# Moving the score, value and x-transpose steps of three attention blocks to other slots of the feed-forward loop

## The chip, the cores and the metric

The kernel runs on one core of a Trainium2 chip. The metric is the time of one execution in microseconds (us) on the device. The kernel before takes 279.12 us as the median of 3 runs (278.87 to 279.75). One further execution was taken with the hardware profiler; all rows quoted here come from it.

## The reference

Two stages are computed one after the other. The inputs q, k and v have 8 batches, 8 heads, 576 positions and 64 channels.

```python
q_c = q.reshape(B, H, nc, chunk, D)          # chunk = 64, so nc = 9
scores = scale * np.matmul(q_c, k_c.transpose(0, 1, 2, 4, 3))
scores = scores - np.max(scores, axis=-1, keepdims=True)
attn = np.exp(scores)
attn = attn / (np.sum(attn, axis=-1, keepdims=True) + 1e-09)
out = np.matmul(attn, v_c)
...
x = np.ascontiguousarray(attn_out.transpose(0, 2, 1, 3)).reshape(B * S, H * D)
h = np.maximum(x @ w_in, 0.0)
return (h * h @ w_out).astype(np.float32)
```

Attention is local to chunks of 64 positions. Its result x has 4608 rows of 512 numbers and goes through a feed-forward network of 2048 hidden units with the square of a relu.

## The kernel before, in words

The 4608 rows are cut into 18 groups of 256 rows, each of four chunks. Two groups make a block, so block n holds groups 2n and 2n+1; there are 9 blocks, 0 to 8. Every step is written in Python, so the program that the engines get is one long list for each of them, and each engine works through its own list from front to back.

For a group the attention consists of three steps on TensorE, which the plan in the code names SC, AV and XT:

- **SC** (`scores`, line 464): 32 matmuls of 64x64 write the scores of the group into a PSUM tile of two banks (line 483). One ScalarE instruction of 128x1024 takes the exponential into an SBUF tile `e` (line 494).
- **AV** (`values`, line 496): two halves, t = 0 and t = 1. In each, 16 matmuls of 64x65 multiply `e` with v (line 510) into a PSUM tile. The 65th column is the sum of the exponentials. VectorE takes its reciprocal (line 442) and multiplies (line 443) into the SBUF tile `x`.
- **XT** (`transpose_x`, line 530): 8 TensorE transposes of 128x128 (line 540) write x transposed into a PSUM tile, and ScalarE copies it into `xT` (line 545), which the feed-forward network reads.

All these PSUM tiles come from `att_bank` (line 358), which in this part of the kernel hands out two tiles in turn, `ps_att` and `ps_att2`. A step that gets a tile has to wait until the last reader of that tile is done: the exponential for scores, the product on line 443 for values, the copy on line 545 for transposes. For the two groups of block 2 and of block 4 the order is SC, SC, AV, AV, XT, XT; in block 3 the first group has its XT before the second has its AV.

Ahead of SC stand the casts of q and k to bf16 (`C`, lines 449 and 454, on GpSimd, for block 4 on ScalarE) and a DMA transpose (`TD`, line 460, issued by SyncE).

The feed-forward network of a block j is `ffn_in(j)` (line 573) and `ffn_out(j)` (line 728). `ffn_in` gives one step for each 128 hidden units: four matmuls into a PSUM tile (line 579), a relu on ScalarE (line 590), and a square, for most steps on VectorE (line 598) and for a few on ScalarE (line 596). Its PSUM tiles come from a pool of four, so a step waits for the relu of the step four before it. In block 1 the two groups go through `ffn_in` apart, 16 steps each of 256 columns; in blocks 2 and 3 together, 16 steps of 512 columns. `ffn_out` multiplies sums and differences of the squares with sums of `w_out`, in 14 steps of 8 matmuls of 128x256 (line 780). VectorE makes the sums (line 614), ScalarE copies intermediate products away (`keep`, line 840), and VectorE adds a kept one to a finished one and stores the sum (`summed_out`, line 820, whose add is again line 614).

The loop `for j in range(QUADS)` (line 1004) weaves both together: after each step of the network, called a slot, it issues what a dictionary `plan` holds for that slot. So with j = 1 the network of block 1 runs while the attention of block 2 is done, with j = 2 the attention of block 3, with j = 3 that of block 4. For j = 1 slots 0 to 31 are `ffn_in` and 32 to 45 `ffn_out`. For j = 2 slots 0 to 15 are `ffn_in`, slots 16 to 18 hold no work of TensorE, and 19 to 32 are `ffn_out`. For j = 3 the loop has the 16 slots of `ffn_in` alone. From block 4 on a different scheme follows (`run`, line 1160), which is not changed.

Of the kernel before, what the change touches and what calls it, by code (L numbers as in the profile page):

```python
# [144 lines left out]
def kernel(  # L145
# [174 lines left out]
    def go(pieces):  # L320
        for f in pieces:
            f()
# [250 lines left out]
    def ffn_in(j, parts):  # L573
        gT = gT_main.rearrange("p (u h) (f t) -> p u h f t", u=2, f=4)
        xT = xTs[j]
        for u, (c, n, ft) in enumerate((c, n, ft) for c, n, fts in parts for ft in fts):
            h = ps_ffn.tile([128, 512], FP32, name="ps_ffn")
            for dt in range(n_dt):
                nc.tensor.matmul(  # L579
                    out=h[:, 0:n],  # L580
                    lhsT=w_in_bf[:, dt, ft * 128:(ft + 1) * 128],
                    rhs=xT[:, c // 128:(c + n) // 128, dt, :],
                    start=(dt == 0), stop=(dt == n_dt - 1))
            if n == 512 or u % 2 == 0:
                state["rl"] = state.get("rl", -1) + 1
                rl_tile = relu_sb[state["rl"] % 4]
                if j < 3:
                    rl_tile = rl_tile.bitcast(BF16)
            rl = rl_tile[:, u % 2 * 512:] if n < 512 else rl_tile
            nc.scalar.activation(out=rl[:, 0:n], in_=h[:, 0:n], func=AF.Relu)  # L590
            u0, u1 = c // GT, (c + n) // GT
            dst = gT[:, u0:u1, ft // 4, ft % 4, :]
            src = rl[:, 0:n].rearrange("p (u t) -> p u t", t=GT)
            if (n == 512 and ft in SQUARES_ON_ACT) or (
                    n < 512 and ft in (12, 3)) or (j == 0 and u == 0):
                nc.scalar.activation(out=dst, in_=src, func=AF.Square)
            else:
                nc.vector.tensor_tensor(out=dst, in0=src, in1=src, op=ALU.mult)  # L598
            yield
# [16 lines left out]
    def summed(out, in0, in1, op=ALU.add):  # L616
        return lambda *_: add(out, in0, in1, op)
# [277 lines left out]
    def ffn_out_by_ft(j):  # L895

        n_tt = BT // 128
        o_ps = [ps_ffn.tile([128, d_model], FP32, name="ps_ffn") for _ in range(n_tt)]

        def mm(tt, ft):  # L900
            nc.tensor.matmul(  # L901
                out=o_ps[tt],
                lhsT=g_piece(j, tt // 2, ft // HF, ft % HF // 4)[
                    :, ft % 4, tt % 2 * 128:tt % 2 * 128 + 128],
                rhs=w_out_bf[:, ft, :],
                start=(ft == 0), stop=(ft == n_ft - 1))


        for ft in range(n_ft - 4):
            for tt in range(n_tt - 1 if ft == 0 else n_tt):  # L910
                mm(tt, ft)
                if ft == 1 and tt == n_tt - 2:
                    mm(n_tt - 1, 0)
            yield
        for tt in range(n_tt):
            for ft in range(n_ft - 4, n_ft):
                mm(tt, ft)
            o_sb = ffn_pool.tile([128, d_model], FP32, name="o_sb", bufs=4)
            nc.scalar.copy(out=o_sb, in_=o_ps[tt])
            b, s0 = chunks[blocks[j][tt // 2]][0]  # L920
            t0 = b * S + s0 + tt % 2 * 128
            nc.gpsimd.dma_start(out=out[t0:t0 + 128, :], in_=o_sb)
            yield
# [3 lines left out]
    def pieces(grps):  # L927
        for g in grps:
            yield from qk_pieces(g)
        for g in grps:  # L930
            yield from v_pieces(g)

    SC, AV, XT = scores, values, transpose_x
    TD = transpose_qk_dma
# [69 lines left out]
    for j in range(QUADS):  # L1004
        grps, nxt, far = blocks[j], blocks[j + 1], blocks[j + 2]
        plan = {}

        def at(slot, f, *x):
            plan.setdefault(slot, []).append((f, x))

        if j == 0:
            loads, go_slots = pieces(far), range(17)
            at(28, summed(b11_p_b21, b11, b21))
            for slot, f in ((24, TA), (27, SC), (29, AV), (31, XT)):
                at(slot, f, nxt[0])
            at(31, TQ, nxt[1])
            at(31, TK, nxt[1])
            at(31, summed(b22_m_b21, b22, b21, ALU.subtract))
            phases = [first_ffn_in, ffn_out_by_ft(0)]
        elif j == 1:  # L1020
            loads, go_slots = itertools.chain(*map(qk_pieces, far)), range(26, 48)
            for slot, f in ((3, SC), (6, AV), (12, XT)):
                at(slot, f, grps[1])
            for i, g in enumerate(nxt):
                for slot, f in ((16 + 4 * i, C), (21 + 4 * i, TD), (36 + i, SC), (38 + 2 * i, AV),
                                (41 + 2 * i, XT)):
                    at(slot, f, g)
            for i, g in enumerate(far):
                at(36 + 4 * i, C, g)
                at(42 + 3 * i, TD, g)  # L1030
            at(2, summed(b12_p_b21, b12, b21))
            at(12, summed(b11_m_b12, b11, b12, ALU.subtract))
            at(20, summed(b12_p_b22, b12, b22))
            out_j = ffn_out(1)
            for i in (20, 27, 29, 31):
                at(i, lambda: next(out_j)())
            phases = [ffn_in(1, [(0, 256, FT_ORDER), (256, 256, FT_ORDER)]), out_j]
        else:
            out_j = ffn_out(j)
            for i in (14, 15):  # L1040
                at(i, lambda: next(out_j)())
            phases = [ffn_in(j, [(0, BT, range(n_ft))])]
            if j == 2:
                loads, go_slots = itertools.chain(*map(v_pieces, nxt), pieces(far)), [
                    *range(16), *range(27, 36)]
                slots = {SC: (6, 10), AV: (12, 22), XT: (15, 28), CQ: (20, 22), CK: (21, 24), TD: (24, 26)}
                for f in (CQ, CK, TD):
                    for i, g in enumerate(far):
                        at(slots[f][i], f, g)
                phases.append(out_j)  # L1050
            else:
                loads, go_slots = pieces(far), range(11)
                at(11, C, far[0])
                at(13, CQ, far[1])
                at(13, TD, far[0])
                slots = {SC: (2, 4), AV: (7, 10), XT: (13, 15)}
            for f in (SC, AV, XT):
                for i, g in enumerate(nxt):
                    at(slots[f][i], f, g)
            if j == 2:  # L1060
                for i, f in enumerate((summed(a21_p_a22, a21, a22),
                                       summed(a12_m_a21, a12, a21, ALU.subtract),
                                       summed(a11_p_a21, a11, a21))):
                    at(1 + 2 * i, f)
        slot = 0
        for phase in phases:
            for _ in phase:
                if slot in go_slots:
                    for f in loads:
                        f()  # L1070
                        break
                for f, x in plan.get(slot, []):
                    f(*x)
                slot += 1
        assert all(x < slot for x in plan), (j, slot, sorted(plan))
        if j < QUADS - 1:
            go(loads)
# [19 lines left out]
    for j in range(QUADS, n_blk):  # L1097
        if j == QUADS:
            n = 14 - LEAD
            slots = [1 + 19 * i // n for i in range(n)]  # L1100
            assert len(slots) == n
        else:
            slots = [s for s in range(4, 20) if s % 16 not in NO_OUT]
# [119 lines left out]
```

## Time and profile before

| | us |
|---|---|
| median of 3 runs | 279.12 |
| profiled execution, its own time | 278.37 |
| its span, first to last instruction | 276.6 |
| TensorE busy | 265.3 (96%) |
| VectorE busy | 199.3 (72%) |
| ScalarE busy | 170.1 (61%) |
| GpSimd busy | 90.7 (33%) |

A row of the timeline reads: start in us from the span's start, duration in us, engine, line of the kernel, operation, output and input, how many instructions are merged in the row, and in brackets how long the engine was idle before it and what ended that. PE is TensorE, PEld its weight loads, DVE is VectorE, ACT is ScalarE, POOL is GpSimd, SP is SyncE. The ends of matmuls are modelled, so the start of the next row tells more than the duration. The 1.8 us between the profiled execution's time and its span lie before the first and behind the last instruction.

### The profile page before, as it was taken

How to read it: one execution, taken by the hardware profiler on the slowest of the kernel's cores; microseconds unless marked ns; L12 is line 12 of the kernel's file. 1: busy time of each engine (PE TensorE's matmuls, PEld its weight loads, DVE VectorE, ACT ScalarE, POOL GpSimd, SP SyncE). 2: the span in 40 equal slices, each digit the busy share in tenths (PEclk: the TensorE clock that was granted, in tenths of full speed). 3: DMA queues.
4: the chain of work that ended last, by engine and by line, in shares of the span. 5: the costliest groups of instructions: out<-in, count | busy, mean ns of one | idle time of the engine just before them, and what ended most of it. 6: DMA issues, size and time to landing. Idle time of an engine off the chain costs nothing.

```text
span 276.6 us, 7949 instructions
## 1 busy us (share of the span) xinstructions
PE 265.3 (96%) x3274; PEld 203.9 (74%) x3277; DVE 199.3 (72%) x365; ACT 170.1 (61%) x302; POOL 90.7 (33%) x122
## 2 busy tenths in 40 slices
PE   2889999999999999999999999999999999999994
PEld 2764445888774588447888888888898888888884
DVE  1457415999538692599989998799679877994852
ACT  1657514894458883867678765566856664756430
POOL 2048734350270012140245224551434312431600
PEclk9999999999999999999999999999999999999999
DMA  7999999999999999998999999697995330220223
GB/s 216 260 373 383 366 318 262 325 209 162 278 209 206 245 246 231 285 240 121 229 228 199 217 236 198 116 214 198 254 195 162 78 76 2 89 62 9 71 83 114
DMA packets 133943, 55.07 MB, mean 199 GB/s; under 512 B 102160, under 2 KB 129808, under 8 KB 133904
## 3 DMA queue, kind: packets, MB, share of 16 engines
q1 hardware_dynamic: 131136, 46.02, 70.9%
q0 software_dynamic: 2624, 8.39, 9.7%
q8 instruction: 26, 0.43, 0.6%
q10 hardware_dynamic: 144, 0.13, 0.1%
q14 instruction: 13, 0.11, 0.1%
HBM read 36.70 MB, written 9.44 MB: 167 GB/s over the span
## 4 chain that ended last, share of the span: by engine, by line
PE 82%; DVE 8%; DMA 4%; SPq 4%; issue 1%; ACT 0%; POOL 0%
PE ps_ffn L657 23%; PE ps_out L780 22%; PE ps_ffn L579 13%; PE ps_ffn L780 12%; PE ps_ffn L901 5%; DVE gT L598 4%; PE ps_att L510 2%; DMA w_st<-in_moe_w_in_dram 2%; PE ps_att L483 2%; PE ps_att L540 2%; DMA qkT<-qkb 2%; SPq L266 1%; SPq L308 1%; SPq L312 1%; DVE x L443 1%
## 5 line engine op out<-in xcount | busy, mean ns | idle before, releaser
L579 PE MATMUL ps_ffn<-xT,w_in_bf 128*128 128x512 bf16 (+1 forms) x328 | 58.0, 333 | 0.1
L780 PEld LDWEIGHTS <-w_st 128*128 128x128 bf16 x512 | 48.8, 98 | 6.6 <-DVE w_st L614 0.5
L665 DVE CUSTOM_DVE_ANT_0 relu<-ps_ffn,w_st 128x512 f32<-128x512 f32 x60 | 39.3, 685 | 12.8 <-PE ps_ffn L657 11.4
L598 DVE TENSOR_TENSOR gT<-relu 128x256 bf16<-128x256 bf16 (+2 forms) x68 | 34.6, 543 | 18.0 <-ACT relu L590 17.5
L579 PEld LDWEIGHTS <-w_in_bf 128*128 128x128 bf16 x328 | 31.1, 98 | 21.4 <-POOL w_in_bf L334 0.2
L590 ACT ACTIVATE relu<-ps_ffn 128x256 bf16<-128x256 f32 (+2 forms) x82 | 39.5, 502 | 10.3 <-PE ps_ffn L579 9.6
L657 PE MATMUL ps_ffn<-qk_st,w_in_bf 128*128 128x256 bf16 x240 | 35.3, 273 | 0.0
L657 PEld LDWEIGHTS <-w_in_bf 128*128 128x128 bf16 x320 | 30.6, 98 | 4.0 <-issue 0.3
L809 POOL DMA_DIRECT2D out_dram<-o_sb x24 | 17.6, 733 | 44.7 <-DVE o_sb L614 24.6
L780 PEld LDWEIGHTS <-gT 128*128 128x128 bf16 x296 | 28.6, 98 | 3.3
L780 PE MATMUL ps_out<-w_out_bf,w_st 128*128 128x256 bf16 x240 | 30.8, 273 | 0.0
L699 ACT ACTIVATE w_st<-ps_ffn 128x512 f32<-128x512 f32 x20 | 11.9, 598 | 27.5 <-PE ps_ffn L657 27.5
L443 DVE TENSOR_TENSOR x<-ps_att,recs 128x512 bf16<-128x512 f32 x36 | 24.9, 692 | 1.2
L657 PEld LDWEIGHTS <-qk_st 128*128 128x128 bf16 x240 | 22.6, 98 | 2.9
L676 POOL TENSOR_TENSOR qk_st<-relu 128x512 bf16<-128x512 f32 x10 | 10.3, 1034 | 41.6 <-DVE relu L665 38.1
L657 PE MATMUL ps_ffn<-xT,qk_st 128*128 128x256 bf16 x160 | 23.9, 273 | 0.0
L494 ACT ACTIVATE e<-ps_att 128x1024 bf16<-128x1024 f32 x18 | 18.4, 1023 | 8.6 <-PE ps_att L483 8.6
L676 POOL TENSOR_TENSOR gT<-relu 128x512 bf16<-128x512 f32 x10 | 10.3, 1033 | 36.9 <-DVE relu L665 36.9
L449 POOL CAST qkb<-qk_st 128x1024 bf16<-128x1024 f32 x12 | 14.8, 1236 | 13.3 <-DMA qk_st<-in_q_dram 13.3
L674 ACT ACTIVATE gT<-relu 128x512 bf16<-128x512 f32 x28 | 17.7, 631 | 0.0
L780 PE MATMUL ps_ffn<-w_out_bf,w_st 128*128 128x256 bf16 x144 | 17.7, 273 | 0.0
L614 DVE TENSOR_TENSOR w_st<-gT,w_st 128x1024 bf16<-128x1024 bf16 x26 | 17.5, 708 | 0.0
(92 smaller groups left out, 430.5 us busy)
## 6 DMA issues: line engine op xcount, KB each, us to landing
qk_st<-in_q_dram SPq DMA_DIRECT2D x16, 512.0 KB, 5.8
out_dram<-o_sb POOLq DMA_DIRECT2D x28, 256.0 KB, 3.9
qk_st<-in_k_dram SPq DMA_DIRECT2D x24, 256.0 KB, 5.3
ve_sb<-in_v_dram SPq DMA_DIRECT2D x32, 128.0 KB, 3.9
w_st<-in_moe_w_in_dram SPq DMA_DIRECT2D x8, 512.0 KB, 6.0
w_st<-in_moe_w_out_dram SPq DMA_DIRECT2D x8, 512.0 KB, 5.4
vo_sb<-in_v_dram SPq DMA_DIRECT2D x24, 128.0 KB, 3.3
qk_st<-in_k_dram SPq DMA_DIRECT2D x4, 512.0 KB, 5.9
```

What stands on the lines that cost most here:

```text
L443: nc.vector.tensor_tensor(out=x, in0=o[:, :, :, 0:D], in1=rec.to_broadcast([128, 2, n, D]), op=ALU.mult)
L494: nc.scalar.activation(out=e_out, in_=s_in, func=AF.Exp, scale=scale)
L579: nc.tensor.matmul(out=h[:, 0:n], lhsT=w_in_bf[:, dt, ft * 128:(ft + 1) * 128], rhs=xT[:, c // 128:(c + n) // 128, dt, :], start=(dt == 0) ...
L590: nc.scalar.activation(out=rl[:, 0:n], in_=h[:, 0:n], func=AF.Relu)
L598: nc.vector.tensor_tensor(out=dst, in0=src, in1=src, op=ALU.mult)
L614: nc.vector.tensor_tensor(out=out, in0=in0, in1=in1, op=op)
L657: nc.tensor.matmul(out=bank[:, f * GT:(f + 1) * GT], lhsT=a[:, dt, ft * 128:(ft + 1) * 128], rhs=b[:, :, dt, :], start=(first and f == 0 a ...
L665: nc.vector._custom_dve(TENSOR_ADD_SAT, out=out, in0=in0, in1=in1, s0=BIG, s1=0.0)
L674: engine.activation(out=dst, in_=r, func=AF.Square)
L676: engine.tensor_tensor(out=dst, in0=r, in1=r, op=ALU.mult)
L780: nc.tensor.matmul(out=out_ps, lhsT=lhsT, rhs=b[:, i, :], start=(first and i == 0 and (last or t == 0)), stop=(i == HF - 1), skip_group_ch ...
L809: dma.dma_start(out=out[t0:t0 + GT, col:col + HD].rearrange("(t p) d -> p t d", p=128), in_=o_sb.rearrange("p (t d) -> p t d", d=HD))
```

## The change

Only numbers of slots are changed. The x transpose of group 3 (the second of block 1) goes from slot 12 to 13 of j = 1. In block 2, SC goes from slots 36 and 37 to 37 for both groups, AV from 38 and 40 to 39 and 41, XT from 41 and 43 to 42 and 44. In block 3, SC goes from slots 6 and 10 to 10 for both, the first AV from 12 to 13, and the first XT from 15 to 16; slot 16 holds no network work on TensorE. In block 4, SC goes from slots 2 and 4 to 2 for both, and the first AV from 7 to 6. The lists of SyncE and GpSimd are the same in both programs; those of TensorE, ScalarE and VectorE hold the same instructions in another order.

```diff
         elif j == 1:
...
-            for slot, f in ((3, SC), (6, AV), (12, XT)):
+            for slot, f in ((3, SC), (6, AV), (13, XT)):
                 at(slot, f, grps[1])
             for i, g in enumerate(nxt):
-                for slot, f in ((16 + 4 * i, C), (21 + 4 * i, TD), (36 + i, SC), (38 + 2 * i, AV),
-                                (41 + 2 * i, XT)):
+                for slot, f in ((16 + 4 * i, C), (21 + 4 * i, TD), (37, SC), (39 + 2 * i, AV),
+                                (42 + 2 * i, XT)):
                     at(slot, f, g)
...
-                slots = {SC: (6, 10), AV: (12, 22), XT: (15, 28), CQ: (20, 22), CK: (21, 24), TD: (24, 26)}
+                slots = {SC: (10, 10), AV: (13, 22), XT: (16, 28), CQ: (20, 22), CK: (21, 24), TD: (24, 26)}
...
-                slots = {SC: (2, 4), AV: (7, 10), XT: (13, 15)}
+                slots = {SC: (2, 2), AV: (6, 10), XT: (13, 15)}
             for f in (SC, AV, XT):
                 for i, g in enumerate(nxt):
                     at(slots[f][i], f, g)
```

## The prediction, made before the changed kernel was run

> **What bounds the kernel now.** First the page's busy times, then a table by stage (stretch, length, busy time of PE, PEld, DVE, ACT and POOL with instruction counts, granted clock, DMA share, GB/s).
>
> ```profile
> PE 265.3 (96%) x3274; PEld 203.9 (74%) x3277; DVE 199.3 (72%) x365; ACT 170.1 (61%) x302; POOL 90.7 (33%) x122
> ```
>
> ```profile
> 64.30:79.95 15.65, 15.38 (x259) 12.88 (x257) 10.05 (x23) 6.30 (x9) 4.02 (x5) 1.00 1.07 227
> 79.95:95.70 15.75, 15.75 (x170) 7.48 (x168) 9.72 (x20) 12.62 (x21) 2.94 (x4) 1.00 1.02 217
> ...
> 126.40:272.00 145.60, 145.60 (x1772) 125.19 (x1770) 120.26 (x217) 91.01 (x162) 49.54 (x56) 1.00 0.62 144
> ```
>
> TensorE is the bound. Behind 126.40 it is busy 145.60 of 145.60 us, so what the edited stages gain or lose goes to the end unchanged. The edited stages are the first (block 2's attention in the second half of block 1's network), the second (block 3's, up to its first x transpose) and, from 109.04 to 126.40, block 4's. No matmul is added or removed; a gain or loss can only be a TensorE wait or a change between 128x128 and 64x64 matmuls. So I replay each stage with the rows' durations: TensorE, ScalarE and VectorE each work through their lists in order, and an instruction starts when its inputs and its PSUM tile are there. The lists of SyncE and GpSimd don't change.
>
> **Price of joining two score groups.** The matmul rows give it.
>
> ```profile
> 79.95 6.21 PE L579 MATMUL ps_ffn<-xT,w_in_bf 128*128 128x512 bf16 x28
> 86.08 0.45 PE L483 MATMUL ps_att<-qkT 64*64 64x64 bf16 x32
> 86.46 3.63 PE L579 MATMUL ps_ffn<-xT,w_in_bf 128*128 128x512 bf16 x16
> 90.02 0.45 PE L483 MATMUL ps_att<-qkT 64*64 64x64 bf16 x32
> 90.40 1.90 PE L579 MATMUL ps_ffn<-xT,w_in_bf 128*128 128x512 bf16 x8
> ```
>
> Seven steps and one entry into the 64x64 form take 86.08 - 79.95 = 6.13 us, four and one 90.02 - 86.46 = 3.56; so a step is 0.866 us (3 steps: 2.57) and an entry 0.09. A score group is 0.38 us from its start to the next row. The last of 32 matmuls starts 0.34 us behind the first (0.45 less a matmul's own 0.11 of tail), so a second group behind the first costs 0.34 and no entry: joining saves about 0.09 + 0.04 = 0.13 us a pair. No row shows 64 such matmuls in a row; between nothing saved and the whole 0.47 us of a group gone I stay at 0.13, which the rows carry.
>
> **Block 1's last x transpose and block 2 (j = 1).** The second score group waits for a DMA now.
>
> ```profile
> 70.47 0.44 PE L483 MATMUL ps_att<-qkT 64*64 64x64 bf16 x32 [0.27 <-DMA qkT<-qkb]
> ```
>
> TensorE is there at 70.20. The DMA transpose hangs on SyncE's list alone, so it lands at 70.42 in the new order too. Joining brings TensorE there earlier, by 0.13. The transpose of group 3, at its old place:
>
> ```profile
> 55.41 0.77 PE L540 MATMUL ps_att<-ident,x 128*128 128x128 bf16 x8
> 56.02 0.27 PE L579 MATMUL ps_ffn<-xT,w_in_bf 128*128 128x256 bf16 x1
> ```
>
> It holds TensorE 0.61 us, of which 0.16 is a wait for x (a transpose without one takes 0.45, next rows): one step later that goes. But only two steps of 0.44 us are left ahead of slot 16, which reads the result, and the copy on ScalarE ends 1.66 us behind the transpose's start (0.65 + 1.01, rows below): 0.45 + 0.88 leaves it 0.38 short with the 0.05 of the signal. So between -0.16 and +0.22, and with joining between -0.29 and +0.09: all ahead of 70.47, worth nothing. What covers it is that DMA; were it 0.3 us sooner, it would show at most 0.3 of gain.
>
> ```profile
> 74.55 1.05 PE L780 MATMUL ps_ffn<-w_out_sum,gT 128*128 128x256 bf16 x8
> 75.55 0.62 PE L540 MATMUL ps_att<-ident,x 128*128 128x128 bf16 x8
> 76.01 1.91 PE L780 MATMUL ps_ffn<-w_out_bf,gT 128*128 128x256 bf16 x16
> 77.75 0.61 PE L540 MATMUL ps_att<-ident,x 128*128 128x128 bf16 x8
> ```
>
> ```profile
> 74.80 0.69 DVE L443 TENSOR_TENSOR x<-ps_att,recs 128x512 bf16<-128x512 f32 x1
> 75.41 0.20 DVE L442 RECIPROCAL recs<-ps_att 128x8 f32<-128x8 f32 x1
> 75.64 0.69 DVE L443 TENSOR_TENSOR x<-ps_att,recs 128x512 bf16<-128x512 f32 x1
> 76.25 0.68 DVE L614 TENSOR_TENSOR o_sb<-ps_ffn,kept 128x512 f32<-128x512 f32 x1
> 77.96 0.69 DVE L614 TENSOR_TENSOR o_sb<-ps_ffn,kept 128x512 f32<-128x512 f32 x1 [1.03 <-PE ps_ffn L780]
> ```
>
> ```profile
> 78.40 1.01 ACT L545 COPY xT<-ps_att 128x1024 bf16<-128x1024 bf16 x1 [1.18 <-PE ps_att L540]
> ```
>
> A step of `ffn_out` is 0.87 us (76.01 to 77.75 is two). From the scores' end at 70.84 the new order is: two steps, 72.58; values of group 4 (entry 0.09, 0.39), 73.06; two steps, 74.80; values of group 5, 75.28; one step, 76.15. Now the transpose of group 4 wants the PSUM tile that held the first values of group 5. VectorE frees it, but `summed_out` of slot 41 now stands ahead of group 5's products on VectorE's list, where it stood behind them. That add needs the matmuls of slot 41 (modelled end 74.98; the row at 77.96 starts 0.04 behind such an end), so: add at 75.03, reciprocal 0.61 later, product 0.23 after that with 0.69, done 76.56. The transpose starts at 76.62 (now 75.55, 0.06 behind 75.49), 0.45 late. Then 0.46, two steps, the last transpose at 78.82; 0.45 and one step, 80.14. The first step of `ffn_in(2)` needs ScalarE's copy: 0.65 behind the transpose (78.40 less 77.75) and 1.01 long, done 80.48. In the old order two steps stand between, and the copy is done 0.54 us ahead of need. So `ffn_in(2)` starts at 80.53 and not at 79.95: **+0.58**. If the add slips behind the products: +0.15; if the copy waits for its neighbours on ScalarE, +0.9.
>
> **Block 3 (j = 2).** The first x transpose, and ScalarE and VectorE ahead of it:
>
> ```profile
> 95.22 0.64 PE L540 MATMUL ps_att<-ident,x 128*128 128x128 bf16 x8
> 95.70 0.38 PE L780 MATMUL ps_ffn<-w_out_sum,gT 128*128 128x256 bf16 x2
> ```
>
> ```profile
> 90.13 0.60 ACT L590 ACTIVATE relu<-ps_ffn 128x512 bf16<-128x512 f32 x1 [0.27 <-PE ps_ffn L579]
> 90.76 0.63 ACT L596 ACTIVATE gT<-relu 128x512 bf16<-128x512 bf16 x1
> 91.29 1.00 ACT L494 ACTIVATE e<-ps_att 128x1024 bf16<-128x1024 f32 x1
> 92.19 1.07 ACT L590 ACTIVATE relu<-ps_ffn 128x512 bf16<-128x512 f32 x2
> ```
>
> ```profile
> 92.82 0.91 DVE L598 TENSOR_TENSOR gT<-relu 128x512 bf16<-128x512 bf16 x2 [2.50 <-ACT relu L590]
> ```
>
> ```profile
> 94.72 0.69 DVE L443 TENSOR_TENSOR x<-ps_att,recs 128x512 bf16<-128x512 f32 x1
> ```
>
> On the old clock: 11 steps and an entry, scores at 89.57, both groups to 90.29 (now 90.40); three steps and an entry, values of group 6 at 92.98 to 93.37; two steps, transpose due at 95.10 (now 95.22). ScalarE: the relu of slot 10 starts 1.07 behind its matmuls, 89.68, its square 90.31, then both exponentials, 90.84 and 91.74 (0.90 apart, as 91.29 to 92.19). The relus of slots 11, 12, 13 follow at 92.64, 93.13, 93.62: nearly one exponential late. VectorE squares each 0.63 behind its relu, and slot 13's square, formerly behind the products, now stands ahead: 94.25 to 94.68. From the last square's end (93.73) to both products' end (95.41) is 1.68 us now, so x of group 6 is done at 96.36 instead of 95.41. The transpose, which sat only two steps behind its values, waits for it: end 96.36 + 0.05 + 0.24 = 96.65 against 95.70 now. **+0.95**. It can be as little as -0.12 (if x came in time, the earlier position alone) and as much as +1.3 (another square's 0.35 in front). VectorE's sums for `ffn_out(2)` move by 0.5 and TensorE by 0.95, so no new wait follows there; the DMA transposes for block 4 hang on casts that move with it.
>
> **Block 4 (j = 3).**
>
> ```profile
> 112.32 1.02 ACT L494 ACTIVATE e<-ps_att 128x1024 bf16<-128x1024 f32 x1
> ```
>
> ```profile
> 116.41 2.73 DVE L598 TENSOR_TENSOR gT<-relu 128x512 bf16<-128x512 f32 x3 [0.71 <-ACT relu L590]
> ```
>
> ```profile
> 120.14 0.69 DVE L443 TENSOR_TENSOR x<-ps_att,recs 128x512 bf16<-128x512 f32 x1
> ```
>
> ```profile
> 111.72 0.45 PE L483 MATMUL ps_att<-qkT 64*64 64x64 bf16 x32
> ...
> 120.88 0.22 PE L510 MATMUL ps_att<-ve_sb,e 64*64 64x65 bf16 x2 [0.47 <-DVE x L443]
> ...
> 121.14 1.04 PE L579 MATMUL ps_ffn<-xT,w_in_bf 128*128 128x512 bf16 x4
> ```
>
> Here the second values wait 0.47 us for their tile and the instructions behind them start 0.25 us after that group resumes. New order: scores 111.72 to 112.44; four steps and an entry, values of group 8 at 116.00 to 116.39; four and an entry, values of group 9 at 119.94 to 120.33. ScalarE: exponentials at 112.32 and 113.22, relu of slot 3 at 114.12, its square 114.75, relus at 115.28, 115.78, 116.28 (the steps from start to start as in block 3: 0.90, 0.63, 0.53, 0.50). VectorE: three squares of 0.69 us, started 0.61 apart, the last from 117.13; reciprocal 117.74; both products done at 119.50 (product to product 0.84). The tile is free 0.44 us ahead of need, because only three squares and not four are in front, so the wait goes. 120.33 against 121.14: **-0.80**. What is late next is the x of group 9, done 123.01, ahead of its transposes. With the wait moved instead of removed the term is -0.14.
>
> **Sum.** 0.58 + 0.95 - 0.80 = +0.73 us on the profiled execution's 278.37. That one is 0.75 below the median of 279.12; I add the difference to the median: 279.85 us.
>
> **A rule weighed.** In block 3 and 4 two exponentials now follow each other on ScalarE, 1.9 us, while TensorE makes both groups' scores in 0.72. The Trainium skill, "TensorEngine Tiling (Array Packing)", Performance Considerations, says that tiling speeds up TensorE but not the emptying of PSUM, which may become the bottleneck. By that rule ScalarE would hold the network's PSUM tiles; by the rows the relu of slot 11 ends at 93.2 and its tile is wanted by slot 15 at 94.23, so TensorE would not wait for a tile and the sum stays +0.73. The rule's own outcome is rival 3.
>
> **Rivals.**
> 1. Block 4's wait stays: VectorE is over 0.44 us later than replayed at 119.50 (a fourth square, or relus 0.5 later). Price 0.66: 280.5, slower. For it: VectorE's three squares took 2.73 us at 116.41, waiting for relus. Against: those relus now come earlier.
> 2. x of group 6 comes in time: if VectorE reaches it 1.3 us sooner, block 3 gives -0.12 and the sum is -0.34: 278.8. If in block 2 the add doesn't hold the transpose either (+0.15 there), 278.35, and with the DMA 0.3 sooner 278.05, faster. For it: TensorE waited only about 0.03 us at this transpose. Against: that is no slack.
> 3. ScalarE's backlog reaches the network's PSUM tiles, once it is over 1.0 us later than replayed. One wait of about 0.9 us, the length of an exponential, in each of blocks 3 and 4: 279.85 + 1.8 = 281.6, slower. Against: the margins of 1.0 us and, in block 4, 1.7.
>
> **How the numbers follow.** About 0.3% (0.84 us) is what a measurement of this kernel tells from no change: 278.28 to 279.96 is the same. Forecast 0.52 (its own range 279.3 to 280.4; 0.32 of the chance below 279.96, 0.20 above), rival 1 0.21, rival 2 0.20 (half of it the same, half faster), rival 3 0.07. Faster 0.10, same 0.42, slower 0.48. The range 278.4 to 280.7 leaves out rival 3 and the faster half of rival 2, 0.17 together.
>
> **What would show it.** Right: a span near 277.3; the wait on the DMA transpose about 0.5 us with the same start of block 2's second scores; a transpose row (line 540) of about 0.9 to 1.1 us idle or stretched near 95 to 97, releaser the product of line 443; TensorE idle ahead of `ffn_in(2)`, released by ScalarE's copy; no idle at block 4's second values. Wrong: no gap at those two transposes, a gap at line 579 released by a relu, or the 0.47 us still there.

## The result and the profile after

The changed kernel takes 279.98 us as the median of 22 runs (278.53 to 282.94). The kernel before, run beside it, takes 278.57 us (22 runs, 277.38 to 280.27). The ratio is 1.0056 with a 95% interval of 1.0039 to 1.0073, or +1.56 us (1.09 to 2.03). The change makes the kernel about 0.6% slower. Medians count all runs, and the ratios are not their quotients. A ratio, here and below, and the difference in us worked out from it, leave out executions over 1.5% above the fastest of their kernel; of the profiled ones two are left out so, the second of the whole change (283.35 us) and the first with the cast held back (288.32 us).

The profiled execution of the changed kernel took 278.7 us. The page's span and busy times are nearly those of before:

```profile
span 276.9 us, 7951 instructions
...
PE 265.2 (96%) x3274; PEld 204.1 (74%) x3277; DVE 199.6 (72%) x365; ACT 170.3 (62%) x302; POOL 89.3 (32%) x122
```

The span grew by 0.3 us where the runs grew by 1.56. So this pair of traces shows less of the loss than the runs do, and it has to be read by stages. The waits of TensorE from 45 to 130 us (releaser, us in total, times, longest) are others than before:

```profile
PE ps_att L540 <- DVE x L443: 1.1, 3, 0.4
PE ps_ffn L579 <- ACT xT L545: 0.5, 2, 0.2
```

Before there were 0.47 us at block 4's second values and 0.27 us at a DMA transpose. Both are gone from the list, and x transposes and copies of x stand in their place. The rows of TensorE's timeline around them:

```profile
57.33 7.15 PE L579 MATMUL ps_ffn<-xT,w_in_bf 128*128 128x256 bf16 x64 [0.23 <-ACT xT L545]
...
64.31 1.91 PE L780 MATMUL ps_ffn<-w_out_bf,w_st 128*128 128x256 bf16 x16
...
69.64 0.87 PE L483 MATMUL ps_att<-qkT 64*64 64x64 bf16 x64
70.45 1.92 PE L780 MATMUL ps_ffn<-w_out_bf,w_st 128*128 128x256 bf16 x16
...
76.30 0.62 PE L540 MATMUL ps_att<-ident,x 128*128 128x128 bf16 x8 [0.31 <-DVE x L443]
...
80.21 9.66 PE L579 MATMUL ps_ffn<-xT,w_in_bf 128*128 128x512 bf16 x44 [0.23 <-ACT xT L545]
89.80 0.71 PE L483 MATMUL ps_att<-qkT 64*64 64x64 bf16 x64
...
95.81 0.40 PE L540 MATMUL ps_att<-ident,x 128*128 128x128 bf16 x4 [0.38 <-DVE x L443]
96.65 0.40 PE L540 MATMUL ps_att<-ident,x 128*128 128x128 bf16 x4 [0.44 <-DVE x L443]
96.88 1.04 PE L780 MATMUL ps_ffn<-w_out_sum,gT 128*128 128x256 bf16 x8
```

Block 2's transpose waits 0.31 us and the copy behind the last transpose 0.23. Block 3's transpose waits twice, once for each half of x. The stage windows after (length, then busy time of PE, PEld, DVE, ACT, POOL) have the same columns as before:

```profile
80.21:96.88 16.67, 15.84 (x168) 7.40 (x168) 10.05 (x20) 13.14 (x22) 2.04 (x3) 1.00 0.95 219
110.06:126.69 16.63, 16.62 (x210) 8.11 (x208) 11.69 (x21) 13.54 (x22) 4.33 (x5) 1.00 0.99 245
126.40:272.00 145.60, 145.59 (x1775) 125.25 (x1773) 120.43 (x218) 91.41 (x162) 49.61 (x56) 1.00 0.66 146
```

Block 3's stage went from 15.75 to 16.67 us, block 4's from 17.36 to 16.63. The long rest is again busy throughout.

For the experiments each trace is cut at the starts of TensorE rows: from the row behind block 2's second scores to `ffn_in(2)` (9.11 us before, 9.76 after), from there to `ffn_in(3)` (29.09 and 29.85), from there to `ffn_out(3)` (17.36 and 16.63), and on to the next network's first matmul on line 657 (3.52 and 3.53).

### The profile page after: what moved, and what is told of

The parts are those of the page before. It is cut to its first block, busy times and chain, and to the rows that moved or that the text cites. A ratio compares the mean times of both kernels' runs of the same rounds, so it can differ in the third digit from the quotient of the medians.

```text
span 276.9 us, 7951 instructions
## 1 busy us (share of the span) xinstructions
PE 265.2 (96%) x3274; PEld 204.1 (74%) x3277; DVE 199.6 (72%) x365; ACT 170.3 (62%) x302; POOL 89.3 (32%) x122
## 4 chain that ended last, share of the span: by engine, by line
PE 89%; SPq 3%; ACT 2%; DMA 2%; DVE 1%; issue 1%; DVEq 0%
PE ps_ffn L657 23%; PE ps_out L780 22%; PE ps_ffn L579 18%; PE ps_ffn L780 13%; PE ps_ffn L901 5%; PE ps_att L510 2%; PE ps_att L540 2%; PE ps_att L483 2%; DMA vo_sb<-in_v_dram 2%; SPq L266 1%; ACT relu L590 1%; SPq L308 1%; SPq L312 1%; DVE x L443 1%; ACT xT L545 1%
## 5 line engine op out<-in xcount | busy, mean ns | idle before, releaser
L545 ACT COPY xT<-ps_att 128x1024 bf16<-128x1024 bf16 x11 | 11.1, 1012 | 11.5 <-PE ps_att L540 11.4
L449 POOL CAST qkb<-qk_st 128x1024 bf16<-128x1024 f32 x12 | 12.8, 1069 | 15.6 <-DMA qk_st<-in_q_dram 15.6
```

The costliest lines, as they stand in the source:

```text
L545: copy(out=dst, in_=psb)
```

## The experiments

**One block's slots at a time.** The three parts were run apart, and then the whole change again. Block 2 alone:

```diff
-                for slot, f in ((16 + 4 * i, C), (21 + 4 * i, TD), (36 + i, SC), (38 + 2 * i, AV),
-                                (41 + 2 * i, XT)):
+                for slot, f in ((16 + 4 * i, C), (21 + 4 * i, TD), (37, SC), (39 + 2 * i, AV),
+                                (42 + 2 * i, XT)):
```

> Only block 2's slots are changed (scores 37 and 37, values 39 and 41, transposes 42 and 44). Theory (late x and late copy): +0.58 us on the kernel before; in its profile the first x transpose of block 2 waits about 0.3 to 0.45 us for a product of line 443 and ffn_in(2) about 0.2 to 0.4 us for the copy of line 545. Rival (the part of the measured loss that the profile of the changed kernel does not show, some 0.9 us, belongs to this block, for instance to the DMA transpose ahead of its scores): +1.3 us or more, while the profile still shows +0.6.

It took 280.01 us against 278.6; the ratio is 1.0042 (1.0005 to 1.0079), +1.17 us (0.14 to 2.2), which takes in the rival's +1.3 as well. Its stage takes 9.77 us, that of the whole change 9.76: block 2's own stage costs 0.65 us whatever stands around it. Block 4 kept its old slots here and waited again, in rows of VectorE, GpSimd and TensorE:

```profile
117.73 2.95 DVE L598 TENSOR_TENSOR gT<-relu 128x512 bf16<-128x512 f32 x3 [0.71 <-ACT relu L590]
```

```profile
119.11 1.03 POOL L449 CAST qkb<-qk_st 128x1024 bf16<-128x1024 f32 x1 [6.95 <-DMA qk_st<-in_q_dram]
```

```profile
122.43 0.22 PE L510 MATMUL ps_att<-ve_sb,e 64*64 64x65 bf16 x2 [0.51 <-DVE x L443]
```

Block 3 alone:

```diff
-                slots = {SC: (6, 10), AV: (12, 22), XT: (15, 28), CQ: (20, 22), CK: (21, 24), TD: (24, 26)}
+                slots = {SC: (10, 10), AV: (13, 22), XT: (16, 28), CQ: (20, 22), CK: (21, 24), TD: (24, 26)}
```

> Only block 3's slots are changed (scores 10 and 10, first values 13, first transpose 16). Theory: +0.95 us; the first x transpose waits twice for line 443, 0.8 us together. Rival 2 of the prediction (x comes in time): -0.12 us. Rival (the unseen part belongs here): +1.8 us.

It took 279.51 us, ratio 1.001 (0.9976 to 1.0043), +0.28 us (the medians lie 0.9 us apart); by time alone this can't be told from nothing, and the rival's +1.8 lies outside the interval. From `ffn_in(2)` to `ffn_in(3)` its trace takes 29.85 us, as in the whole change: +0.76. Block 4's old slots, however, took 16.67 us here and had no wait. The rows of VectorE and of GpSimd show why:

```profile
118.08 2.08 DVE L598 TENSOR_TENSOR gT<-relu 128x512 bf16<-128x512 f32 x3 [0.71 <-ACT relu L590]
```

```profile
121.59 1.03 POOL L449 CAST qkb<-qk_st 128x1024 bf16<-128x1024 f32 x1 [9.08 <-DMA qk_st<-in_q_dram]
```

In the kernel before, a cast ran beside the three squares that stand ahead of the second values' product:

```profile
116.67 1.33 POOL L449 CAST qkb<-qk_st 128x1024 bf16<-128x1024 f32 x1 [5.84 <-DMA qk_st<-in_q_dram]
```

There the three squares took 2.73 us (the row at 116.41, shown in the prediction), in the block 2 run 2.95, and here, where the cast came later, 2.08. In these rows GpSimd starts the cast when q's load for group 10 lands, so whether the old slots wait depends on the load and not on the slots alone. Block 4 alone:

```diff
-                slots = {SC: (2, 4), AV: (7, 10), XT: (13, 15)}
+                slots = {SC: (2, 2), AV: (6, 10), XT: (13, 15)}
```

> Only block 4's slots are changed (scores 2 and 2, first values 6). Theory: -0.80 us, and the 0.47 us wait ahead of the second values gone. Rival 1 of the prediction (the wait stays): -0.14 us. Rival (the unseen part belongs here): 0 to +0.1 us though the profile shows the gain.

It took 278.8 us, ratio 0.9987 (0.9957 to 1.0017), -0.36 us: a gain of 0.80 is inside the interval, none at all too. The stage takes 16.64 us, and 0.43 us of wait for a sum of VectorE followed behind it (line 780; 4.10 us where before has 3.52). Here a later cast met the squares ahead of that sum:

```profile
125.73 2.72 DVE L598 TENSOR_TENSOR gT<-relu 128x512 bf16<-128x512 f32 x3
```

```profile
126.45 1.46 POOL L449 CAST qkb<-qk_st 128x1024 bf16<-128x1024 f32 x1 [1.29 <-DMA qk_st<-in_q_dram]
```

The whole change once more:

> The changed kernel as a whole, once more beside its parts. Theory of waits seen in the first profile: +0.6 us. First measurement: +1.56 us. If the three parts are independent, their sum is this kernel's difference; if the sum falls short, a part of the loss needs two of them together or the transpose of group 3.

It took 280.64 us, ratio 1.0047 (1.0016 to 1.0077), +1.31 us. Blocks 2 and 3 take in this second trace what they took in the first (9.76 and 29.85). Block 4's 17.48 us in it are not used below.

Four traces with the old slots and this network (before, block 2 alone, block 3 alone, and the late transposes below) have 17.36, 17.58, 16.67 and 17.63 us in this stage; two with the new ones (the change, block 4 alone) 16.63 and 16.64. But a cast that comes late is paid behind the stage, as in the block 4 run. Counted up to line 657, the four have 20.88, 21.10, 20.28 and 21.15 us, mean 20.85, and the two 20.16 and 20.74, mean 20.45. That puts the gain near 0.4 us, on few traces.

**Holding the cast back.** If the cast decides, keeping it behind group 9's attention must take the wait from the old slots. A small GpSimd copy that reads group 9's x stands ahead of the cast for this, first into a new tile of 128x1, with the old and with the new block 4 slots:

```diff
+                held = const_pool.tile([128, 1], BF16, name="held")
+                at(11, lambda: nc.gpsimd.tensor_copy(out=held, in_=state["x", nxt[1]][:, 1, n_hp - 1, 1, D - 1:D]))
```

> The kernel before, with the GpSimd casts of group 10 and 11 held back until the second x of block 4 is done (one GpSimd copy of 128x1 that reads that x, queued ahead of them). Theory (the 0.47 us wait in the first profile came from a GpSimd cast running beside VectorE's squares, and only when the load lands then): block 4's stage, from the first matmul of ffn_in(3) to the first of ffn_out(3), takes 16.65 us in place of 17.36 to 17.58, without a wait for line 443; the casts may then slow the squares of the last steps and cost up to 0.6 us behind it. Rival (the wait is the order's own: four squares ahead of the products): 17.3 us and the wait still there.

> The same hold with block 4's new slots alone. Theory: 16.62 us for the stage, so the new slots gain only 0.03 us over the old ones once the cast is out of the way. Rival (the new order gains by itself): 0.7 to 0.8 us less than the old order with the same hold.

They took 286.73 and 286.25 us (6 runs each), ratios 1.0192 (1.0135 to 1.0249) and 1.0222 (1.0155 to 1.029). Neither theory had this. The loss begins before the copy runs: in the second of the two the first network matmul starts at 19.00 us, in the kernels without the added tile at 17.03 to 17.57. The loads of k took longer from issue to landing (5.0 to 5.9 us in those kernels), in the DMA issues of the kernel before and of the second of the two (count, KB each, median us):

```profile
qk_st<-in_k_dram SPq DMA_DIRECT2D x24, 256.0 KB, 5.3
```

```profile
qk_st<-in_k_dram SPq DMA_DIRECT2D x24, 256.0 KB, 6.4
```

The repeated pair below has the copy too and starts its first network matmul at 17.57 and 17.26 us, so it was the added tile, not the copy, that disturbed these two. They are not read for block 4. They were repeated with the copy going into a column of the identity matrix's first version, which is no longer read at that point:

```diff
+                at(11, lambda: nc.gpsimd.tensor_copy(
+                    out=ident_f32[:, 0:1], in_=state["x", nxt[1]][:, 1, n_hp - 1, 1, D - 1:D]))
```

> The hold of the GpSimd casts once more with the old slots, this time written into a tile that is there already (the f32 identity, which nothing reads any more), so that no tile is added and no other address moves. Theory: the loads land as in the kernel before, block 4's stage (first matmul of ffn_in(3) to first of ffn_out(3)) takes 16.65 us with no wait for line 443 at its second values; behind it up to 0.6 us are lost to the casts. Rival (the wait is the order's own): 17.3 us.

> The same with block 4's new slots. Theory: 16.62 us, 0.03 less than with the old slots, if the DMA transpose of group 9 has landed by the joint scores; if it lands late, a wait of up to 1.8 us ahead of them that the old slots would have had two steps more to hide. Rival (the new order gains by itself): 0.7 us less than with the old slots.

The times are 279.79 us, ratio 1.0041 (1.0009 to 1.0073), and 279.63 us, ratio 1.0042 (1.0008 to 1.0076). With the cast held, the old slots take 16.67 us and the new ones 16.45: they differ by 0.22 us and not by 0.73, and no value step waits. Up to line 657 they take 21.65 and 21.58 us, so with the cast out of the way the order itself is worth 0.2 us at most. But the hold cost more than expected. The casts now run beside VectorE's sums for `ffn_out(3)`; GpSimd, VectorE and TensorE with the old slots:

```profile
125.02 1.50 POOL L454 CAST qkb<-qk_st 128x1024 bf16<-128x1024 f32 x1
```

```profile
125.54 1.52 DVE L614 TENSOR_TENSOR w_st<-gT 128x1024 bf16<-128x1024 bf16 x1
...
128.53 0.69 DVE L614 TENSOR_TENSOR w_st<-gT 128x1024 bf16<-128x1024 bf16 x1
```

```profile
129.28 1.48 PE L780 MATMUL ps_out<-w_out_bf,w_st 128*128 128x256 bf16 x12 [1.31 <-DVE w_st L614]
```

A sum of this shape takes 1.52 us beside a cast and 0.69 without one. TensorE waits 1.31 us, and from `ffn_out(3)` to line 657 it is 4.98 us instead of 3.52. The slowing was not removed, only moved to another victim.

**Short squares.** For the last network of the loop the relus can be stored as bf16, as for the others. Squares then take 0.43 us instead of 0.69, so the old slots should have slack:

```diff
-                if j < 3:
+                if j < 4:
```

> The kernel before, with the relu of block 3's network kept in bf16, as the blocks ahead of it have it, so that VectorE's squares take about 0.42 us and not 0.69. Theory (VectorE is late by squares plus a cast): even with a cast beside them three or four squares end over 0.8 us sooner, the stage takes 16.65 us with any landing of the load, and the kernel is 0.0 to 0.7 us faster than before, depending on how many of its runs have the wait. Rival (the wait has nothing to do with the squares): 17.4 us, same time.

> The same short squares with block 4's new slots alone. Theory: 16.62 us for the stage and no measurable difference from the short squares with the old slots. Rival (the new order gains by itself): faster than them by 0.7 us.

With the old slots it took 278.66 us, ratio 1.0011 (0.9978 to 1.0044); the stage is 16.67 us without a wait, 0.7 less than in the trace of before, and yet the time is the same. In this trace the cast came only when the three squares were done, so it does not show what short squares do beside a cast:

```profile
118.78 0.43 DVE L598 TENSOR_TENSOR gT<-relu 128x512 bf16<-128x512 bf16 x1 [0.47 <-ACT relu L590]
```

```profile
119.77 1.03 POOL L449 CAST qkb<-qk_st 128x1024 bf16<-128x1024 f32 x1 [7.94 <-DMA qk_st<-in_q_dram]
```

With the new slots it took 278.9 us, ratio 0.9987 (0.9957 to 1.0016). The two ratios differ by 0.24%, 0.7 us, and their intervals overlap, so the times do not separate the theory from the rival. The stage with the new slots is 18.41 us, for a new reason in TensorE's rows:

```profile
112.43 0.45 PE L483 MATMUL ps_att<-qkT 64*64 64x64 bf16 x32
114.66 0.44 PE L483 MATMUL ps_att<-qkT 64*64 64x64 bf16 x32 [1.78 <-DMA qkT<-qkb]
```

Joined scores need the second group's DMA transpose two steps sooner, and here it was late. The DMA issues from 100 to 116 us of this kernel have, as the median from issue to landing:

```profile
qkT<-qkb SPq DMA_TRANSPOSE x2, 8.6
```

In the same window of the kernel before it is 5.9 us:

```profile
qkT<-qkb SPq DMA_TRANSPOSE x2, 5.9
```

In the old order the two steps, 1.73 us, would have stood ahead of these scores and covered nearly all of that wait. It is one trace of the four that have joined block 4 scores and no hold.

**Later transposes.** If a transpose only comes too early for x, moving it back must return the loss; if the order of ScalarE's list makes VectorE late, the wait moves on. Block 2 has its x transposes at slots 43 and 44, block 3 its first one at slot 20, all else in these blocks as in the change (without the move of group 3's transpose), and block 4 as before:

```diff
-                                (41 + 2 * i, XT)):
+                                (43 + i, XT)):
...
-                slots = {SC: (6, 10), AV: (12, 22), XT: (15, 28), CQ: (20, 22), CK: (21, 24), TD: (24, 26)}
+                slots = {SC: (10, 10), AV: (13, 22), XT: (20, 28), CQ: (20, 22), CK: (21, 24), TD: (24, 26)}
```

> Blocks 2 and 3 with the joint scores and later values as in the change, but with the x transposes moved further back: block 2's to slots 43 and 44 in place of 42 and 44, block 3's first to slot 20 in place of 16. Theory of the late x: from the end of block 2's scores to ffn_in(2) 9.21 us (9.11 in the kernel before, 9.76 in the changed one; what stays is the wait for ScalarE's copy), from ffn_in(2) to ffn_in(3) 28.97 us (29.09 before, 29.85 changed), no wait at line 540. Rival (the loss comes with the joint scores or the later values themselves): 9.7 and 29.7 us.

It took 279.73 us, ratio 1.0032 (1.0002 to 1.0063), +0.89 us. Block 2's stage is 9.28 us with no wait of a transpose: 0.48 of its 0.65 us comes back, and what remains is the copy ahead of `ffn_in(2)`. Block 3 takes 29.79 us, nearly all of its loss. TensorE and VectorE there:

```profile
98.48 1.05 PE L780 MATMUL ps_ffn<-w_out_bf,w_st 128*128 128x256 bf16 x8 [0.95 <-DVE w_st L614]
```

```profile
97.14 0.69 DVE L443 TENSOR_TENSOR x<-ps_att,recs 128x512 bf16<-128x512 f32 x1
97.75 0.68 DVE L614 TENSOR_TENSOR w_st<-gT 128x1024 bf16<-128x1024 bf16 x1
```

Now `ffn_out(2)` waits 0.95 us for its second operand, a sum that stands behind the products on VectorE's list. So in block 3 the place of the transpose isn't the cause. The relus, squares, products and sums are all late, and whichever TensorE needs first collects the wait. The joint scores and the later first values were not run apart, so how the loss divides between them is not shown.

**A candidate.** Block 3 as in the last run together with the bf16 relus, all else as before:

> What the runs point to: the kernel before, with block 3's joint scores and its first transpose at slot 20, and block 3's relu kept in bf16 for shorter squares; blocks 2 and 4 as before. Theory: 0.12 us from block 3 in every execution and up to 0.7 us in those where a cast runs beside the squares: 0.1 to 0.5 us faster than before in the median, at the edge of what can be measured. Rival: no difference, as with the short squares alone.

It took 279.07 us, ratio 1.0004 (0.9976 to 1.0033). Block 3 gained nothing: from `ffn_in(2)` to `ffn_in(3)` it is 29.80 us, with a wait of 0.94 us for the same sum as in the last run. And this time the cast met a short square, in rows of VectorE, GpSimd and TensorE:

```profile
119.68 1.23 DVE L598 TENSOR_TENSOR gT<-relu 128x512 bf16<-128x512 bf16 x1 [0.47 <-ACT relu L590]
```

```profile
119.60 1.03 POOL L449 CAST qkb<-qk_st 128x1024 bf16<-128x1024 f32 x1 [6.88 <-DMA qk_st<-in_q_dram]
```

```profile
122.65 0.22 PE L510 MATMUL ps_att<-ve_sb,e 64*64 64x65 bf16 x2 [0.34 <-DVE x L443]
```

The square took 1.23 us and not 0.43, the value step waited 0.34 us, and the stage took 17.20 us. So short squares make the wait smaller, but do not take it away "with any landing of the load", as was expected of them. No version tried is measurably faster than the kernel before.

## Why the prediction was right in sign and short in size

The forecast was +0.73 us and the measurement is +1.56 (1.09 to 2.03). That the predicted time of 279.85 stands near the measured 279.98 is in part luck: the kernel before, in this larger set of runs, takes 278.57 and not 279.12 us.

- **Block 2, predicted +0.58: right, with its mechanism.** All three traces with these slots have +0.65. The add stood ahead of the products as replayed:

```profile
74.71 0.69 DVE L614 TENSOR_TENSOR o_sb<-ps_ffn,kept 128x512 f32<-128x512 f32 x1 [0.23 <-PE ps_ffn L780]
75.55 0.69 DVE L443 TENSOR_TENSOR x<-ps_att,recs 128x512 bf16<-128x512 f32 x1
```

  The product ends at 76.24 and the transpose starts at 76.30. Moving the transpose back returned 0.48 us and left the copy's wait.

- **Block 3, predicted +0.95: right in mechanism, 0.2 too much net.** The stage up to the transpose's end grew by 0.92 us. The two exponentials and what came behind them:

```profile
91.07 1.92 ACT L494 ACTIVATE e<-ps_att 128x1024 bf16<-128x1024 f32 x2
92.88 1.57 ACT L590 ACTIVATE relu<-ps_ffn 128x512 bf16<-128x512 f32 x3
```

```profile
93.51 1.40 DVE L598 TENSOR_TENSOR gT<-relu 128x512 bf16<-128x512 bf16 x3 [3.41 <-ACT relu L590]
```

  Behind it 0.16 us came back (13.18 us instead of 13.34). The old order had a small wait for a sum in `ffn_out(2)`, which the prediction had not seen inside a merged row of TensorE; the weight loads of the kernel before show it:

```profile
97.60 0.77 PEld L780 LDWEIGHTS <-w_st 128*128 128x128 bf16 x8 [0.27 <-DVE w_st L614]
```

  The net is +0.76.

- **Block 4, predicted -0.80: the step that failed.** The trace of the change has -0.73 with the wait gone, but the other traces show that this isn't the worth of the change. The prediction took the three squares' 2.73 us as waiting for relus, and with it the 0.47 us of wait as a property of the slots. It was a cast on GpSimd beside them, at a time that the load sets. Without a cast there, the old slots ran without a wait, in 16.67 us (block 3 alone, and the hold into the old tile), and the new ones took 16.45 to 16.64. With the new slots a late cast took 0.43 us behind the stage in one trace of two. Counted up to line 657 the mean of the few traces is -0.4. In the sum, 0.65 + 0.76 - 0.4 = +1.0 us, just below the measured interval.

- **Joining two score groups, predicted to save 0.13: 0.2.** The rows of block 4:

```profile
112.74 0.71 PE L483 MATMUL ps_att<-qkT 64*64 64x64 bf16 x64
113.38 0.82 PE L579 MATMUL ps_ffn<-xT,w_in_bf 128*128 128x512 bf16 x3
```

  The 64 matmuls hold TensorE 0.64 us to the next row, where 0.72 was expected. The rows under the 0.13 were misread twice. Three steps in 2.57 us are 0.857 us each and not 0.866; but three steps ahead of the first x transpose take 2.60 us (92.62 to 95.22), so 0.866 holds. And in the trace the last of 32 score matmuls starts 0.25 us behind the first, not 0.34.

- **Group 3's transpose, predicted worth nothing behind the DMA: not told apart.** The copy's wait is there, 0.23 us at 57.33. The wait for the DMA, now expected at about 0.5 us, is not listed at all, but the joined scores at 69.64 hold TensorE 0.81 us, where block 4's hold it 0.64. From the first row on line 579 to the row behind block 2's second scores it is 53.26 us against 53.42. That stretch varies by more than 2 us from trace to trace (last point), and this move was not run alone.

- **Rivals.** ScalarE's backlog did not reach the network's PSUM tiles (rival 3): no wait at line 579 has a relu as releaser. By the rule of the Trainium skill, "TensorEngine Tiling (Array Packing)", Performance Considerations, the emptying of PSUM might have become the limit; here the backlog showed one engine further on, in VectorE's products. Rival 2, x of group 6 in time, falls with the two waits at 95.81 and 96.65. Rival 1, block 4's wait staying, shows in neither of the two traces with the new slots, but in one of them the sum of `ffn_out(3)` was waited for instead.

- **The rest stays open.** The parts measured apart add up to 1.17 + 0.28 - 0.36 = +1.09 us, each uncertain by about 0.8 to 1.0; the whole change measured +1.56 and, the second time, +1.31 (0.45 to 2.15). Between +1.0 by the traces and these lie some tenths. They can hide in a stretch that varies by itself: from the first network matmul to the row behind block 2's second scores, eight traces with block 2's old slots (without the added tile) take 53.08 to 55.39 us and three with the new ones 53.26 to 54.94, both 54.2 in the mean. The first profiles of both kernels, with 53.42 and 53.26, are among the shortest. In this stretch TensorE waits for DMA transposes ahead of block 2's scores, longest in the run with the later transposes:

```profile
71.80 0.44 PE L483 MATMUL ps_att<-qkT 64*64 64x64 bf16 x32 [1.49 <-DMA qkT<-qkb]
```

  So few traces show no sign that the joined scores lengthen it, and do not rule it out. A late DMA transpose ahead of block 4's joined scores (1.78 us in one trace) is another candidate, but how often it occurs was not measured.

## What to carry to other kernels

A duration that is longer than the same instruction's elsewhere in the trace (three squares in 2.73 us, where three take 1.9 to 2.1) may have a neighbour as its cause; look for it before pricing its removal, since here a load decided when that neighbour ran. Two steps that share a serial engine should not be moved together only because TensorE runs them cheaper together: 0.2 us saved on TensorE put 0.9 us of exponential ahead of relus that another engine's products waited behind. A stage that keeps its length in every trace (9.76, 29.85) can be priced from one profile; one that varies (16.67 to 17.63 with the same slots) needs several.

## What the runs showed of the hardware that was not expected

VectorE's operations with both inputs in SBUF are slower beside a GpSimd cast of 128x1024. A sum of 128x1024 takes 0.69 us alone and 1.52 beside a cast (hold with the old slots); three squares take 1.90 us (117.91 in the block 4 run) and 2.72 beside one. The cast, 1.03 us alone, took 1.46 there and up to 1.52 in the holds, but in the block 2 run it kept 1.03 and only the squares were late. VectorE's products of line 443, which read PSUM, kept their 0.69 us: those at 119.30 and 120.14 in the kernel before ran beside a cast of 1.04 us at 119.44. This agrees with the Trainium skill, "SBUF — State Buffer", Who interferes with whom: VectorE shares one pair of SBUF ports with GpSimd, under an exclusive lock.

One more tile of 128x1 in the first pool made the kernel 1.9 to 2.2% slower, with loads of k of 256 KB landing in 6.4 us where all kernels without it have 5.0 to 5.9; the same copy into an existing tile cost 0.4%. A shift of the addresses behind it would fit the Trainium skill, "DMA: Bandwidth & Descriptors", How a descriptor splits into AXI transactions, where a transaction has to start on a 256-byte boundary. No run here varied the size of the tile, so this cause is only argued.
